# The first chunk's x copied on chip, its channels in a new order, and a new order of all tasks

## The chip, the cores and the metric

The kernel runs on one core of one Trainium2 chip. The metric is the device time of one execution in microseconds (us), taken as the median of several runs. A profile is taken of one further execution, and its time stands beside the span that the profile shows. PE is the matmul engine, PEld its loading of weights, DVE the vector engine, ACT the scalar engine, POOL the GpSimd engine, and SP the engine from whose queue the DMA transfers are issued.

## The reference

All arrays are float32. An attention with a recurrent state runs over 768 steps for 4 x 8 pairs of batch and head with 40 channels each; an MLP of 320 to 2048 to 320 follows on its 3072 tokens.

```python
for t in range(S):
    y[:, :, t] = np.einsum('bhd,bhde->bhe', rt, state)
    Sa = np.einsum('bhde,bhe->bhd', state, at)
    state_decay = state * wt[:, :, None, :] - np.einsum('bhd,bhe->bhde', Sa, bt)
    state = state_decay + np.einsum('bhd,bhe->bhde', vt, kt)
...
x = attn_out.transpose(0, 2, 1, 3).reshape(B * S, H * D)
h = x @ w_in
g = h * (1.0 / (1.0 + np.exp(-1.702 * h)))
out = g @ w_out
```

## The kernel before

**Units and chunks.** Time is cut into 12 chunks of 64 steps. One unit is one chunk of two batches with their 8 heads, so there are 24 units; units 2c and 2c+1 make chunk c. Within a chunk the recurrence is turned into matmuls of 64x64 blocks and the inverse of a triangular matrix.

**One unit.** `load_w` and `load` bring its inputs. `decay` takes logarithms and exponentials of the decays (`FT`, `GT`, `G`, `wch`). `prep` multiplies the inputs with them: `ahT` (L629), `bhT` (L631), `khT` (L634), `kh` and `bh` (L637, from the tile `time`), and makes the masked score blocks A (L648) and RV (L660). `inverse` makes the score N (L697) and inverts by five levels, each a group of matmuls `ps_level` whose result PE needs again after copies and transposes. For units 0 to 3 (`plain_level`) that is one copy of 128x768 (L794) and one transpose of 128x512 (L733) per level. For later units (`level`) it is a copy W (L761), a subtraction E (L763), a transpose ES (L712) and a spread EX (L717 on ACT, L719 on DVE or POOL). Then come the copies Tc (L807), a last transpose and spread into T, the small products `ps_Q` and `ps_T21`, and T (L840). `solve` forms `ps_B0` and `ps_B1`, the product `ps_X`, M (L917), and `ps_y` with the unit's output and its new state. From unit 2 on the state of the unit two before enters through `zr` (L855), `ps_zT` and `ps_rz`.

**From the attention to the MLP.** `decayed` (L956 to L966) multiplies the unit's output with `FT` into the tile `x`, with 40 channels in partitions 0 to 39 and 40 in 64 to 103. The MLP needs x with channels over the partitions in five blocks of 64 for both of its halves of PE. `part_with` (L971) writes `x` to a tensor in HBM with two transfers, and `get_back` (L977) reads it into both halves of `xT` with two more. `mlp` multiplies: one group `ps_up` is the product of one of five blocks k, for one of two halves m of one of four strips q of w_in. A product of either kind waits for the x of both units of its chunk. After a gelu on ACT (L1000), `ps_down` multiplies with w_out.

**Weights.** Both weight matrices arrive as float64 bits in eight pieces (`weight`, L441), four transfers each. A piece is converted by one step on ACT (L457), three on DVE (L461, L465, L469) and one on POOL (L473). Pieces 0 to 3 are w_in, and piece q serves strip q; 4 to 7 are w_out.

**What sets the order.** Nothing is scheduled at run time. Every task has a number, and the text `ORDER` (L109 to L246) lists all of them: number, engine (p PE, a ACT, d DVE, g POOL, s SP), and the PSUM bank, or for SP a window. Each engine runs its own tasks strictly in that order, so a task that waits holds up all that stand behind it on its engine. A window such as `1s4` makes a transfer wait until all but the last four transfers issued before it have landed (`transfer`, L329); 46 of 269 SP tasks carry one. Where a task may run on several engines, the letter in `ORDER` picks one. All inputs, weights and x go through SP's one queue.

**Numbers of tasks.** 413 transfers are issued on SP. On POOL run 161 products and sums, on DVE 428.

Of the kernel before, what the change touches and what calls it, by code (L numbers as in the profile page):

```python
# [109 lines left out]
0s 8s 1s4 5s 102a 7s 6s 3a 9s 157a 87p0 88p1 10s 89a1 100p2 90a0 95d 13s4 4a 11s 93d 12s 101d2 98p3 2s 94d 97d 17s 103p1 16s 96d  # L110
142p0 15s 104a1 105d1 141p2 143a0 106d 99d3 107p1 144a2 18s4 148g 132p3 108a1 109d1 155p0 45s4 149d 27s 150g 156d0 158p2 14s4
110p1 159a2 160d2 91s4 130p0 161d 19a 24s4 112d1 162p2 111a1 22d 26s4 25s 163a2 113p1 20d 131a0 152g 164d2 34s4 92a 272s 21d
165p0 114a1 151g 271s 147a 153p2 115d1 273s 166a0 167d0 116p1 23g 28a 154d2 262p0 343s 117d1 263p2 133a3 342s 264a2 118d1 168p3
36s 31d 33s 119p1 276g 169a3 170d3 35s 120d1 42s 122a1 171p2 277d 278g 121a 43s 124d1 123a1 126p3 173d2 125a1 127d3 285a 29d
128p1 172a2 44s4 286p3 30d 54s4 37a 174p2 129d1 32g 51s4 288d3 134p1 178a2 146s4 175d2 145s 265a0 135d1 176a 187p0 289d 136p1
275s4 179a2 266g 61s 38d 138d1 188a0 341s 139s 287a3 181p0 39d 185p3 40d 137a1 177a2 290p1 313d 180a2 182a0 53s4 280g 279g 274s
186a3 183p2 292d1 281p0 291a1 333p3 41g 184d2 332p1 282d0 189p2 334a3 60s4 345s 314p0 190d2 316a0 346d 355a 191p3 347d 315d0
193d3 356p2 344s2 62s 140s 194s 195s4 192d3 293p0 335a1 358d2 46a 283p3 359d 317p1 294a0 295d0 349g 318a1 284d3 360p0 269a 348d
350g 296p1 336d 361a0 362d0 319p3 383d 357a2 297a1 298d1 384p0 321p2 49d 320a3 299p1 385a0 47d 322a2 63s4 363p3 300a1 301d1
323d2 386a0 302p1 364a3 365d3 353p0 351p2 306a1 48d 267s3 207p3 52s3 307a1 305d1 208p3 50g 268s3 64a 303d1 209p3 352d2 210p3  # L120
211p3 354d0 308a1 196p2 304a 212p3 65d 197p2 213p3 72s3 214p3 70s3 270d 55a 309p1 337s3 198p2 69s4 366p0 310a1 66d 199p2 367a0
200p2 58d 468p1 201p2 368d0 469a 473s 202p2 476s 203p2 67d 387p0 477s 470a1 490d 204p2 68g 480s 339a 205p2 369p1 388d0 206a2
215p3 371d1 218p0 219p0 56d 472s4 216p3 483g 71s4 220p0 217a3 471d 81s4 221p0 482d 79s 311p2 222p0 370a1 223p0 224p0 312d2 225p0
340d 372p3 229p1 478s4 376a3 230p1 57d 378a3 324p2 560s4 377a3 59g 226p0 78s4 375a3 325d2 231p1 73a 232p1 227p0 373d3 326p2 374d
228a0 389p3 484g 479s3 327d2 338s4 240p0 529d 390a3 481g 328d2 379p3 233p1 380a3 329d 234p1 391p2 485g 241p0 556s4 392d2 80s4
242p0 393d2 74d 486p3 235p1 487d3 530p2 236p1 75d 531a2 381p3 237p1 532a2 330s4 382d3 238p1 76d 491p2 394p3 494a2 493d2 77g
239a1 243p0 395d3 82a 488p1 557s3 396p3 489d1 474a 558s4 83d 331s 251p1 492d2 495d 252p1 84d 85d 253p1 398d3 86g 559s4 548p2
244p0 703s 397d3 549a 570d 553s 245p0 496d 550a2 552s 399d 497a 254p1 551g 554a 498p3 564d 400s 568p2 565g 499a3 246p0 569d2
500d3 563g 247p0 562d 694p2 561g 255p1 248a0 401s2 249d0 475d 256p1 250s 533p3 257p1 534a3 555d 695a 571p0 535p3 573d0 258p1
574a0 698s4 501d 696a2 609d 502g 536a3 537p2 572d0 259a1 576d 566p3 538a2 702s 402p0 575g 567d3 577a 403p0 404p0 539d2 785s3  # L130
700a 405p0 706s 708d 406p0 578p3 407p0 580d3 408p0 260d1 610p2 409p0 581d 709g 410p0 611d2 411p0 612d2 503p1 707d 582g 412a0
424p2 425p2 504d1 704s2 426p2 505d1 427p2 697d 428p2 579d3 613p1 701d 429p2 614a1 583p0 430p2 584a0 506d 431p2 585d0 432p2 507a
782s2 586d 433p2 587d 446p3 434a2 508p1 588p0 509a1 447p3 590d0 589a0 510d1 261s2 413p2 511d 699s 414p2 591d 512a 783s 415p2
592g 416p2 513p0 417p2 514a0 515d0 593p1 516d 418p2 594a1 595d1 419p2 596d 420p2 517a 597d 421p2 422p2 518p0 423a2 435p1 519d0
436p1 521d0 520g 437p1 522d0 438p1 523d0 439p1 440p1 524d0 525p2 716p0 526a2 441p1 717d0 927s 442p1 718d0 527p2 443p1 719d0
444p1 528d2 598p0 721d 445a1 540p2 720d 722g 601d0 603a0 617p1 602d0 541d2 448p3 618a1 604d0 542p2 619d1 599d0 600d 615p1 705s
544d2 449p3 616a1 781s 710d 545g 711d 605p0 723p1 606a0 450p3 607p0 451p3 546s 608d0 930s 452p3 725d1 724d1 620p0 726d 543d2
727a 773p1 453p3 621d0 778s 774a 547s 754d 728p2 622p0 454d3 455d3 729d2 456s 457p3 775a1 776g 730d2 784s 786g 779a 777s 624d0
458p3 623d0 625g 731d 793p1 833d 732a 459p3 733p2 789g 460p3 626s 734a2 794d1 735d2 714p0 790g 736d 461p3 780d 737g 1009s 918p1
755p2 923s 462p3 715d0 756a2 627s 757a2 788d 463p3 738p0 787d 464p3 739a0 740d0 919a 795p2 465d3 758p0 1006s 466d3 798a2 921d  # L140
650p3 467s 759d0 920a1 651p3 924a 928s 796d2 712p1 797d2 652p3 922s 800d 799g 653p3 932d 801a 654p3 834p0 655p3 713d1 656p3
657p3 835d0 760p2 836d0 925d 658p3 761a2 659p3 762p1 660a3 741d 628p0 742d 926s 629p0 630p0 763d1 802p2 764d1 631p0 803a2 804d2
632p0 805d 633p0 806a 743p3 634p0 746d3 635p0 747d3 837p1 931g 748d3 636p0 838a1 1007s 749d3 637p0 807p2 744d3 933g 638a0 639p1
808d2 640p1 791p3 745a 809d2 672p0 810d 792d3 811a 750p2 641p1 751a2 812p3 642p1 813a3 814d3 752p2 643p1 753d2 644p1 815d 645p1
816a 765p3 839p2 766d3 646p1 840a2 647p1 817p3 648p1 818a3 819d3 767p2 820d 649a1 821d 673p0 769d2 929s 768d2 770g 822p3 934d
674p0 825a3 826a3 940p1 827a3 675p0 1151s 828a3 935d 943a1 771s 661p2 823d3 662p2 941d1 1154s 824a 663p2 942d1 997p3 945d 944g
664p2 998a 1002s 978d 938p1 946g 665p2 939d1 666p2 772s 667p2 668p2 829p1 669p2 999a3 1000d 1001s 830d1 670p2 1003a 1011d 676p0
671a2 1004d 831p3 841p1 677p0 832d3 1005s 842d1 936p3 843d1 678p0 937d3 844p2 679p0 845d2 947p1 1010g 680d0 846p3 948a1 681d0
1012d 682s 683p2 847d3 1013g 1008s 848d3 1019p0 1014g 949d1 684p2 1022a0 1230s 849d 1233s 979p3 685p2 980a3 950d 850s 1020d0
981a3 951g 1142p1 1021d0 686p2 1024d 1143a 1147s 1023d 1025g 982p3 1057d 687p2 1152s 952p0 851s 983a3 1145g 688p2 1156d 1146s  # L150
953a0 954d0 984p3 1144a1 955d 1148a 689p2 956d 985a3 1149d 986p0 690p2 987a0 1150s 988d0 957p1 691a2 863p3 958a1 692d2 864p3
959d1 865p3 693s 960d 866p3 961d 1026p0 867p3 1027a0 1028d0 868p3 1029d 1155g 869p3 1157d 1030a 1058p2 870p3 871p3 1059a2 872p3
# [97 lines left out]
def rwkv7_gelu_quick(ctx: ExitStack, tc: tile.TileContext, time_d, v_d, w_d, wc_d, ak_d, b_d, rv_d, w_in, w_out, out):  # L250
# [85 lines left out]
    def of(e):  # L336
        return nc.gpsimd if e == "POOL" else nc.vector
# [812 lines left out]
```

## Time and profile before

| | |
|---|---|
| median of 3 runs | 682.22 us (680.29 to 682.74) |
| the profiled execution | 679.49 us |
| its span from first to last instruction | 677.7 us |
| mean granted clock of PE | 0.994 |
| first matmul, first `ps_up`, last matmul's end | 3.80, 66.48, 673.8 us |
| `ps_y` of unit 0, of unit 1 (starts) | 42.00, 49.54 us |
| PE idle 0 to 66.4, and 66.4 to the end | 21.0, 7.4 us |
| DMA, queue of SP | 66.99 MB, 32.9% of 16 engines' span |

The span is less than the execution's time since the start and the end of the program lie around it. A span's busy shares are means over a head, in which the first two chunks' attention runs without any MLP beside it, and a long middle in which both are mixed. The chain that ended last is on PE for most of the span:

```profile
PE 88%; DMA 6%; DVE 2%; issue 1%; SPq 1%; ACT 1%; DVEq 0%; ACTq 0%
```

### The profile page before, as it was taken

The page shows a single profiled execution, that of the slowest core. Times are in us where ns is not written, and L with a number is a line of the kernel's source. Part 1 is how long each engine was busy: PE and PEld are TensorE (multiplying, and loading weights), DVE is VectorE, ACT ScalarE, POOL GpSimd, SP SyncE. Part 2 cuts the span into 40 slices and gives each one's busy share as a digit, 9 for nine tenths or more (in the row PEclk, how much of TensorE's full clock was granted, in tenths as well). Part 3 has the DMA queues.
Part 4 walks back from the last instruction along what each step waited for, and adds up shares of the span by engine and source line. Part 5 has one row for each costly group of instructions (what it writes and reads, how often), then busy time and mean ns, then how long its engine had stood idle before and what let it go on. Part 6 is the DMA issues. An engine that isn't in the chain of part 4 may idle for free.

```text
span 677.7 us, 42447 instructions
## 1 busy us (share of the span) xinstructions
PE 649.6 (96%) x19616; PEld 568.7 (84%) x19616; DVE 449.7 (66%) x916; ACT 329.1 (49%) x681; POOL 175.7 (26%) x201
## 2 busy tenths in 40 slices
PE   5777999999999999999999999999999999999997
PEld 4667787787999997888888899999889798799896
DVE  5777779777867668757776687868656766675001
ACT  3676745634564655654545445455344454263010
POOL 6541443324123123123113211322411421300000
PEclk9979999999999999999999999999999999999999
DMA  6875753415324314432404513513412411200200
GB/s 208 295 255 160 226 172 97 129 42 152 107 64 131 94 58 124 114 107 65 124 14 131 149 35 108 155 33 107 140 38 62 130 53 45 69 15 14 60 13 21
DMA packets 35473, 69.74 MB, mean 103 GB/s; under 512 B 5472, under 2 KB 14816, under 8 KB 35296
## 3 DMA queue, kind: packets, MB, share of 16 engines
q1 hardware_dynamic: 35216, 66.99, 32.9%
q8 instruction: 154, 2.52, 1.6%
q14 instruction: 23, 0.19, 0.1%
q10 hardware_dynamic: 80, 0.04, 0.0%
HBM read 59.15 MB, written 7.86 MB: 99 GB/s over the span
## 4 chain that ended last, share of the span: by engine, by line
PE 88%; DMA 6%; DVE 2%; issue 1%; SPq 1%; ACT 1%; DVEq 0%; ACTq 0%
PE ps_up L301 31%; PE ps_down L301 29%; PE ps_level L301 8%; PE ps_y L301 5%; PE ps_B L301 4%; PE ps_X L301 2%; PE ps_N L301 2%; PE ps_rz L301 1%; PE ps_RV L301 1%; PE ps_A L301 1%; PE ps_zT L301 1%; SPq L331 1%; DMA w_sb<-in_w_in 1%; PE ps_cum L301 1%; PE ps_T L301 1%
## 5 line engine op out<-in xcount | busy, mean ns | idle before, releaser
L301 PE MATMUL ps_up<-xT_all,w_sb 64*64 64x256 f32 x3840 | 253.3, 377 | 2.1 <-issue 1.3
L301 PE MATMUL ps_down<-w_sb,g 64*64 64x320 f32 (+1 forms) x3200 | 241.5, 419 | 0.2 <-ACT zr L879 0.2
L301 PEld LDWEIGHTS ps_up<-xT_all,w_sb 64*64 64x64 f32 x3840 | 170.8, 133 | 18.8 <-issue 2.1
L301 PEld LDWEIGHTS ps_down<-w_sb,g 64*64 64x64 f32 x3200 | 142.5, 133 | 31.6 <-issue 0.4
L1000 ACT ACTIVATE g<-ps_up 128x1024 f32<-128x1024 f32 x48 | 49.2, 1025 | 46.3 <-PE ps_up L301 45.8
L719 POOL TENSOR_TENSOR EX<-ES,quads 128x512 f32<-128x512 f32 x30 | 39.7, 1324 | 116.4 <-DVE ES L712 77.7
L761 ACT COPY W<-ps_level 128x512 f32<-128x512 f32 x56 | 32.8, 585 | 67.7 <-PE ps_level L301 66.0
L301 PEld LDWEIGHTS ps_level<-W,EX 64*64 64x64 f32 x2560 | 60.0, 134 | 5.4 <-DVE T L840 0.2
L763 DVE TENSOR_TENSOR E<-two,ps_level 128x256 f32<-128x256 f32 x80 | 33.1, 415 | 36.5 <-ACT W L761 32.3
L301 PE MATMUL ps_level<-W,EX 64*64 64x64 f32 (+1 forms) x2560 | 56.8, 217 | 0.0
L717 ACT ACTIVATE EX<-ES,quads 128x256 f32<-128x256 f32 x82 | 37.2, 501 | 31.9 <-DVE ES L712 31.3
L629 POOL TENSOR_TENSOR ak<-ak,FT 128x512 f32<-128x512 f32 x17 | 23.0, 1353 | 77.2 <-DMA ak<-in_ak 54.4
L301 PEld LDWEIGHTS ps_level<-PT,EX 64*64 64x64 f32 x1280 | 30.7, 138 | 11.5 <-DVE EX L733 3.3
L301 PE MATMUL ps_level<-PT,EX 64*64 64x64 f32 (+2 forms) x1280 | 32.5, 234 | 6.9 <-DVE EX L733 5.0
L712 DVE STREAM_TRANSPOSE ES<-E 128x256 f32<-128x256 f32 x80 | 35.3, 443 | 4.4
L301 PE MATMUL ps_y<-RV,kh 64*64 64x104 f32 (+1 forms) x768 | 35.4, 247 | 0.9 <-DVE M L917 0.9
L301 PE MATMUL ps_y<-M,bh 64*64 64x104 f32 (+1 forms) x768 | 35.5, 247 | 0.7 <-DVE M L917 0.5
L901 ACT COPY B<-ps_B 128x416 f32<-128x416 f32 (+1 forms) x35 | 17.2, 493 | 34.4 <-PE ps_B L301 34.2
L301 PEld LDWEIGHTS ps_y<-RV,kh 64*64 64x64 f32 x768 | 29.6, 133 | 3.2 <-DVE M L917 1.5
L917 DVE TENSOR_TENSOR M<-ps_X,later 128x832 f32<-128x832 f32 (+1 forms) x24 | 23.9, 995 | 10.2 <-PE ps_X L301 10.0
L301 PE MATMUL ps_B<-RV,A 64*64 64x104 f32 (+1 forms) x768 | 29.2, 252 | 0.8 <-issue 0.8
L637 POOL TENSOR_TENSOR kh<-time,G 128x320 f32<-128x320 f32 x18 | 16.2, 901 | 51.2 <-PE ps_y L301 34.6
(133 smaller groups left out, 1099.0 us busy)
## 6 DMA issues: line engine op xcount, KB each, us to landing
ak<-in_ak SPq DMA_DIRECT2D x48, 160.0 KB
rv<-in_rv SPq DMA_DIRECT2D x48, 160.0 KB
time<-in_time SPq DMA_DIRECT2D x24, 320.0 KB
xT_all<-x_dram SPq DMA_DIRECT2D x48, 160.0 KB
wc<-in_wc SPq DMA_DIRECT2D x20, 264.0 KB
logw<-in_w SPq DMA_DIRECT2D x24, 160.0 KB
RV<-in_v SPq DMA_DIRECT2D x24, 160.0 KB
b<-in_b SPq DMA_DIRECT2D x48, 80.0 KB
```

Of the source, the lines that this page charges most:

```text
L301: nc.tensor.matmul(o, lhsT, rhs, start=start, stop=True, skip_group_check=True)
L331: begun.append(queue.dma_start(dst, src).ins)
L629: plan.add(R, {"DVE": 690.0, "POOL": 1270.0, "sbuf": True}, lambda t: of(t.engine).tensor_mul(ahT(), ahT(), FT_of(i)), reads=T("ak", "FT") ...
L637: plan.add(R + 4, {"POOL": 870.0, "DVE": 490.0, "sbuf": True}, lambda t, n=n, dst=dst: of(t.engine).tensor_mul(dst(i)[:, :, :D], by_head(t ...
L712: plan.add(rank, dve(256), lambda t: nc.vector.transpose(ES(n), source(t)), writes=[key("ES", n, 6)], **reads)
L717: nc.scalar.activation(dst[:, :, h], ES(n), ACT.Copy, scale=quads[:, h, :1])
L719: of(t.engine).tensor_mul(dst, ES(n).unsqueeze(2).to_broadcast([128, 8, 2, 32]), quads.unsqueeze(1).to_broadcast([128, 8, 2, 32]))
L761: plan.add(rank, any2(512), lambda t: copy(t.engine)(tiles_of(W(n + 1)), blocks(psum(t, ""), 64)), writes=[key("W", n + 1, 5)], pair=pair)
L763: plan.add(rank, dve(256), lambda t: nc.vector.tensor_sub(tiles_of(E(n + 1)), every(two32, [128, 2, 4, 32]), blocks(psum(t, ""), 64)[:, :, ...
L901: plan.add(R, any2(4 * wide), lambda t: copy(t.engine)(dst(), some(psum(t, "")[:, :, :208])), writes=[("Bv", i)] if x and c > 0 else T("B" ...
L917: plan.add(R + 1, dve(8 * wide), lambda t: nc.vector.tensor_tensor(M_of(i)[:, :, :wide].rearrange("p (j b) n -> p b j n", b=2), some(psum( ...
L1000: plan.add(-45, {"ACT": 1030.0, "table": "gelu"}, lambda t: nc.scalar.activation(g_of(c * NQ + q).rearrange("p m r n -> p r m n"), psum(t, ...
```

## The change

Three things change together.

**Channels.** w_in's rows stand in a new order (`order`, L1120): in a block k of 0 to 3, 32 partitions hold channels 0 to 31 of head 2k and 32 those of head 2k+1, and block 4 holds what is left, channels 32 to 39 of all eight heads. So 32 of the 40 channels of `x` go to `xT` without changing their place among 32 partitions.

**x of chunk 0.** `first_x` replaces `decayed` there: two products of 128x256 in place of four of 128x128. Four tasks per unit, on DVE or ACT, copy 32 partitions x 512 numbers each from `x` to `xT` (key `xm`); only block 4, a fifth of the bytes, goes through HBM. Products with k < 4 wait for `xm`, those with k = 4 for `xs`. In the new order the copies of unit 0 run on ACT, those of unit 1 two on DVE and two on ACT. For the other chunks all of x still goes through HBM, but its write takes four transfers instead of two, since block 4 is laid out in pieces of 512 bytes.

**The order of all tasks.** `ORDER` is new from start to end. Unit 0's attention is finished first, then unit 1's; w_in's piece 1 is loaded after the others (0, 2, 3). No SP task carries a window any more. SP issues 457 transfers. Some tasks that may run on several engines move: of 161 products and sums on POOL 80 are left, of DVE's 428 there are now 533 (spreads EX and T on POOL 36 before and 3 after, on DVE 35 and 85; `ahT` on POOL 17 and 3; x of later units on POOL 9 and 0). ACT loads its tables 36 times instead of 30.

```diff
             x = x_of().rearrange("p (n f) b t -> p n b f t", f=2)
             for u, b in product(BITS, BITS):
                 at = slice(4 * u + 2 * b, 4 * u + 2 * b + 2)
-                y = both(i)[:, at, :64] if c > 0 else part(t)[:, u, 2 * b:2 * b + 2, :64]
-                of(t.engine).tensor_mul(x[:, b ^ u, b], y, FT_of(i)[:, at])
+                of(t.engine).tensor_mul(x[:, b ^ u, b], both(i)[:, at, :64], FT_of(i)[:, at])
+
+        def first_x(t):
+
+            x = x_of().rearrange("p (u f) b t -> p b u f t", f=2)
+            y, FT = (v.rearrange("p u (b f) t -> p b u f t", f=2) for v in (part(t)[:, :, :, :64], FT_of(i).rearrange("p (u j) t -> p u j t", u=2)))
+            for b in BITS:
+                nc.vector.tensor_mul(x[:, b, ::1 - 2 * b], y[:, b], FT[:, b])
...
-            plan.add(R + 6, {"DVE": 1000.0}, decayed, reads=T("FT"), writes=T("x"), pair=("y", i))
+            plan.add(R + 6, {"DVE": 800.0}, first_x, reads=T("FT"), writes=T("x"), pair=("y", i))
-        rows = lambda: drams[i].rearrange("(e d j) n -> e d (j n)", e=2, d=D)
+        rows = lambda e, k: drams[i].rearrange("(e q) (k n) -> e q k n", e=2, k=NK)[e, :, k]
+        whole, rest = (lambda e: x_of()[64 * e:64 * e + 32]), (lambda e: x_of()[64 * e + 32:64 * e + D])
...
             for e in BITS:
-                transfer(t, rows()[e], x_of()[64 * e:64 * e + D].rearrange("p j b t -> p (j b t)"))
+                if c > 0:
+                    transfer(t, rows(e, slice(0, 4)).rearrange("q k n -> q (k n)"), whole(e).rearrange("p j b t -> p (j b t)"))
+                transfer(t, rows(e, 4).rearrange("(d j) n -> d j n", j=4), rest(e).rearrange("p j b t -> p j (b t)"))
 
         def get_back(t):
             for h in HALF:
-                transfer(t, xT_of(c)[h, p].rearrange("q k n -> q (k n)"), drams[i].rearrange("(q k) n -> q (k n)", q=64))
...
+                to = xT_of(c)[h, p].rearrange("q k n -> q (k n)")
+                transfer(t, to if c > 0 else to[:, 4 * 128:], drams[i] if c > 0 else drams[i][:, 4 * 128:])
+
+        if c == 0:
+            for h, e in product(BITS, BITS):
+                plan.add(R + 6, {"DVE": 400.0, "ACT": 590.0, "sbuf": True}, lambda t, o=64 * h + 32 * e, e=e: copy(t.engine)(
+                    xT_of(c)[o:o + 32, p, :4].rearrange("q k n -> q (k n)"), whole(e).rearrange("p j b t -> p (j b t)")),
+                         reads=T("x"), writes=[("xT", c), ("xm", (c, p))])
...
-            plan.add(R + q, pe((1, 256)), go, reads=[("xs", (c, p)) for p in BITS] + [("weight", q)],
+            plan.add(R + q, pe((1, 256)), go, reads=[("xs" if c > 0 or k == NK - 1 else "xm", (c, p)) for p in BITS] + [("weight", q)],
...
-    order = [d + D * (e + 2 * j) for e in range(2) for d in range(D) for j in range(H // 2)]
+    order = [(q % 32 if k < 4 else 32 + q % 32 // 4) + D * (q // 32 + 2 * (k if k < 4 else q % 4)) for q in range(64) for k in range(5)]
```

The two orders begin so (the first lines of `ORDER`; the numbers of tasks differ from 102 on, as tasks were added):

```diff
-0s 8s 1s4 5s 102a 7s 6s 3a 9s 157a 87p0 88p1 10s 89a1 100p2 90a0 95d 13s4 4a 11s 93d 12s 101d2 98p3 2s 94d 97d 17s 103p1 16s 96d
...
+0s 5s 6s 7s 102a 8s 161a 9s 3a 1s 10s 87p0 88p1 11s 14s 12s 89a1 13s 345s 90a0 93d 94d 100p2 95d 103p3 97d 4a 96d 98p1 101d2
...
```

More of the change, by code (lines that the diff above doesn't have):

```diff
@@ L114 @@
[L114 to L121, printed above, removed]
@@ L977, in get_back @@
         def get_back(t):
             for h in HALF:
-                transfer(t, xT_of(c)[h, p].rearrange("q k n -> q (k n)"), drams[i].rearrange("(q k) n -> q (k n)", q=64))
-        plan.add(-50, {"SP": 700.0}, part_with, reads=T("x"), writes=T("xd"), size=DM * 512)
-        plan.add(-50, {"SP": 700.0}, get_back, reads=T("xd") + ([("weight", raws.index("x"))] if c in (1, 2) else []), writes=[("xT", c), ("xs", (c, p))], size=2 * DM * 512)
+                to = xT_of(c)[h, p].rearrange("q k n -> q (k n)")
@@ L984, in rwkv7_gelu_quick @@
+        plan.add(-50, {"SP": 1400.0 if c > 0 else 700.0}, part_with, reads=T("x"), writes=T("xd"), size=DM * 512 * (5 if c > 0 else 1) // 5)
+        plan.add(-50, {"SP": 700.0}, get_back, reads=T("xd") + ([("weight", raws.index("x"))] if c in (1, 2) else []),
+                 writes=[("xT", c), ("xs", (c, p))], size=2 * DM * 512 * (5 if c > 0 else 1) // 5)
     g_of = lambda n: buf("g", n, [128, 2, 2, 256])
```

264 lines of the change are left out of this document (136 added, 128 removed).

## The prediction, made before the result

> **What bounds the kernel now.** I read the page's first two parts, then the table of stretches, the waits, the groups and the timeline around the first product of the MLP.
>
> ```profile
> PE 649.6 (96%) x19616; PEld 568.7 (84%) x19616; DVE 449.7 (66%) x916; ACT 329.1 (49%) x681; POOL 175.7 (26%) x201
> PE   5777999999999999999999999999999999999997
> PEclk9979999999999999999999999999999999999999
> DMA  6875753415324314432404513513412411200200
> ```
>
> PE is the bound, except in the first four slices. The table of stretches (length, then busy us of PE, PEld, DVE, ACT, POOL, then clock, DMA share and GB/s) puts a border on it:
>
> ```profile
> 20.00:30.00 10.00, 7.60 (x310) 6.25 (x302) 8.59 (x12) 7.85 (x13) 5.52 (x3) 1.00 0.87 291
> 30.00:40.00 10.00, 7.31 (x237) 6.53 (x239) 7.50 (x14) 7.52 (x23) 5.85 (x3) 0.75 0.93 311
> 40.00:50.00 10.00, 7.75 (x323) 6.57 (x315) 7.54 (x15) 6.88 (x24) 4.16 (x5) 0.91 0.68 217
> 50.00:60.00 10.00, 7.23 (x309) 6.61 (x312) 8.35 (x18) 6.72 (x12) 2.64 (x3) 1.00 0.62 177
> 60.00:66.40 6.40, 4.81 (x244) 4.45 (x248) 4.15 (x7) 3.59 (x9) 0.00 (x0) 1.00 0.44 115
> 66.40:678.00 611.60, 604.18 (x17932) 528.70 (x17922) 403.01 (x836) 289.01 (x580) 147.23 (x147) 1.00 0.31 89
> ```
>
> After 66.4 PE lacks 7.4 us in 611.6, about 4 of them after the last matmul. So a new order can win next to nothing there and can only lose. Before 66.4 PE is busy 45.4 us of 66.4, and even that flatters it. At the rates of the dense stretches its groups there are worth 32: 17 `ps_level` at 0.85, twelve of A, N and RV at 0.47, `ps_cumc` 4 at 0.52, `ps_cum` 4 at 0.27, B 4 halves and one pair at 0.36 and 0.72 each, X 2 at 0.71, y 2 at 1.43, the rest 2. From PE's start at 3.8, some 30 us of the head are waiting. What ends the head is the first `ps_up`, and the timeline (start, us, engine) tells what it waited for:
>
> ```profile
> 52.43 0.86 DVE L962 TENSOR_TENSOR x<-ps_y,FT 128x128 f32<-128x128 f32 x4
> 56.67 0.46 SPq L331 DMA_DIRECT2D x_dram<-x  x1
> 61.39 1.09 SPq L331 DMA_DIRECT2D xT_all<-x_dram  x2
> 66.48 2.48 PE L301 MATMUL ps_up<-xT_all,w_sb 64*64 64x256 f32 x40
> ```
>
> x of unit 1 is ready at 53.3; it lies behind other transfers on SP until 56.7, is written to HBM until about 61.3, read back until about 66.4. That is 13.2 us, in which PE did only what the attention of units 2 and 3 gave it.
>
> **The change, part by part.** Whatever is moved, PE does the same groups of matmuls. So I compare the time of the first `ps_up`, and how much PE work stands ahead of it. By the new order six groups `ps_level` (0.85 each in dense stretches) and one each of A, N, B1, zT (0.47, 0.47, 0.72, 0.32) that stood ahead of it come after it: 7.1, say 7.0 us. New span = new first `ps_up` + 611.2 (677.7 - 66.48) + 7.0 + stalls that are new behind it. The change wins only if `ps_up` comes more than 7 us earlier.
>
> *To unit 0's first level.* b is issued ahead of rv and logw of unit 1 behind time, so N, which began at 11.71 after a wait for b, can start near 9. But on DVE both products with time (L637) now stand ahead of RV, PV and EX. Before they ran at 11.37, just after b; I take time's landing at 10.0 (bounds: 9, with one transfer less ahead of it, and 11.3). Then 0.48 + 0.48 + 0.68 + 0.69 + 0.65 + 0.71 = 3.7 us: the first `ps_level` at 13.8 instead of 14.91.
>
> *Unit 0's levels* no longer alternate with unit 1's. One costs PE 1.1, the ACT copy L794 0.80, the DVE transpose L733 0.71, which the trace runs one after another, with hops 2.75:
>
> ```profile
> L794 ACT COPY PT<-ps_level 128x768 f32<-128x768 f32 x15 | 11.9, 802 | 7.7 <-PE ps_level L301 5.8 <-DVE EX L733 1.2 <-ACT logw L536 0.6
> L733 DVE STREAM_TRANSPOSE EX<-ps_level 128x512 f32<-128x512 f32 x16 | 11.4, 710 | 9.9 <-ACT PT L794 8.8 <-PE ps_level L301 1.1
> ```
>
> The second level starts at 17.5 (rv of unit 1 must land for a matmul in between), the fifth at 25.6 (before: 30.83). Tc and ES in turn (5 x 0.45), the ACT spread (0.9), Q, T21 and T between weight steps of 0.8 bring X to 32.8 (before 38.63), M (1.0, behind one more weight step) to 35.7, y of unit 0 to 35.7-37.1 (before 42.0). Six us won.
>
> *Unit 1* loses them again. Its last level stands behind y of unit 0: 37.2, as before (37.42). On DVE three weight steps and x of unit 0 (39.8) stand ahead of its Tc and ES (41.2); spread to 42.1; Q, QT, T21, T to 44.1; X at 44.2-44.9 (before 48.36). Now M of unit 1 stands on DVE behind wz, bhT, zr, khT and RV of unit 2, whose exponentials ACT ends at 44.8 since it made four copies of x of unit 0 first (4 x 0.59). 0.15 + 0.75 + 0.48 + 0.80 + 0.68 = 2.9: 47.7; M to 48.7; y to 50.2. Ahead of x on DVE stand kh, P21, PV, EX, a weight step and A (0.48 + 0.41 + 0.69 + 0.71 + 0.80 + 0.68 = 3.8): 52.5.
>
> *x.* Four products of 128x128 (276 ns each) become two of 128x256. No row has that from PSUM with FT; nearest is L763, 415 ns. 0.83, no change (bounds 0.55 and 1.1). x of unit 1 is ready at 53.3, as before.
>
> *The copies.* No row copies 32x512. Bounds: 0.20 (L807, 32x64) and 0.585 (L761, 128x512 on ACT); width sets it, so 0.59. Two on DVE, two on ACT behind exponentials and logarithms that end at 53.5: 54.7. What PE still has ahead of it, B0 of unit 2 and RV of unit 3, waits for A (52.5) and is done by 53.9. First `ps_up` at 54.7, with 2 us either way for the eight waits summed.
>
> *Stalls behind it.* zT of unit 3 follows seven products (3.0 us) and needs DVE's zr, which stands behind the copies, two scans (1.4 to 1.5), B, RV, EX: 58.0 against 57.7, 0.4. The block that still goes through HBM (k = 4) is wanted after about 5.3 us, 60.0. Its write is issued at 53.3; ahead of it SP issues loads that can't go before `ps_cum` of unit 3 (48.8). By the rows, the full trip took 4.7 + 5.0 in the head and, later, 4.06 and 3.94 in the chain; a first load of 160 KB landed 2.3 after its issue. So a fifth of the bytes comes between 58.6 (issue 0.7, two trips of 2.3) and 63.0: a stall of 0 to 3. I take 0.6, nearer the small one, as these are small. Together 1.0. The Trainium skill ("DMA: Bandwidth & Descriptors", "Anatomy of one DMA — SWDGE (gpsimd) path") speaks against a large gain here: a transfer costs about 2.0 us whatever its size, so a fifth of the bytes does not take a fifth of the time. By that figure the block would land near 58.4 and the stall be nothing, 0.6 less in the sum; by the head's rows it would be 3. The first load's 2.3 agrees with it, the head's 5.0 doesn't.
>
> *Priced at nothing:* all windows on SP (46 waits for earlier transfers) go, which PE feels only through late loads (a rival below). From chunk 1 on, the write of x takes four issues for two (0.32 each, 0.7 us later); PE hides it by products of the chunk before, as only one wait of 0.6 for x stands in the trace. Spreads, `ahT` and x move from POOL to DVE: 41 + 9 spreads at 0.7, 14 ahT at 0.88, 9 x at 1.1 to 1.45, 11 QT at 0.41 come to 67, less copies W, Tc, zT and others that go to ACT or POOL, about 20; +46 us: DVE goes from 66% to 73%, POOL loses half. PE's matmuls hide it; uncovered, see C. Six more ACT table loads of 1.28 lie on an engine at 49%.
>
> Sum: 54.7 + 611.2 + 7.0 + 1.0 = 673.9 for the span, 3.8 less than 677.7. The profiled execution took 679.49, 1.8 more than its span, and the median of the runs is 682.22: 678.4.
>
> **The rivals.** *A, more is won.* The head waits for loads in the first 17 us, and POOL hardly runs beside DVE any more, which brings DVE products with two SBUF operands from 0.80 (L634) to 0.68. If time and logw land 2 us sooner and this adds 1 to 2, `ps_up` comes at 51 and the time is 674.5. Against it: 311 GB/s at 30-40 leaves little room.
>
> *B, loads too late.* Without windows everything issued lies in one queue. Weight 1's four loads and RV of unit 3 can't be issued before 48.9 and need, at 300 GB/s, till 56; ACT's L457 for weight 1 stands ahead of the zT copies, RV's product on DVE ahead of zr. At the 217 GB/s of 40-50 they land 3 us later, and the k = 4 block with them: 3 to 4 us of PE, all that was won. 682.
>
> *C, slower: DVE decides.* For units 4 to 23, E, ES, spread and ahT now queue on DVE with the rest. Each unit's five levels are a chain between DVE and PE; where it gives the next matmul late, PE stands. It decides from 0.19 us per unit (3.8 / 20); at 0.5 per unit it costs 10: 688. For it: from 100 to 120 DVE is busy 18.0 of 20 already. Against: a spread of 0.70 on DVE is shorter than 1.32 on POOL or 1.0 on ACT, and all of PE's gaps behind 66.4 but the tail sum to 3.5 us at today's 66%.
>
> **How the numbers follow.** Forecast 0.48 (own range 675 to 681.5, from 2 us either way at `ps_up` and 0 to 3 at k = 4), A 0.12, B 0.13, C 0.27. A measurement tells 0.5%, 3.4 us, from no change. Faster by that: A and 0.34 of the forecast, 0.46; within: 0.14 and B, 0.27; slower: 0.27. The range takes in A and most of C: 671 to 688.
>
> **What would show it.** First `ps_up` between 53 and 57; `ps_y` of unit 0 near 36 and of unit 1 near 49; x at 53 with DVE, not PE, in front of it; a wait of `ps_up` for xT_all under 1.5 us; after that PE short of no more than 9 us to the end. I am wrong if x of unit 1 comes before 50 or after 56, if PE's gaps behind 100 us sum to over 8, or if SP's loads end the waits at 55-62.

## The result, and the profile after

The changed kernel takes 725.86 us (median of 6 runs, 722.47 to 727.27) where the kernel before takes 681.63 beside it (680.29 to 684.85): 1.0637 times as long, with a 95% interval of 1.0603 to 1.0670. Forecast were 678.4 and a range of 671 to 688. The profiled execution has a span of 723.7 us, 46 more than before. Two kernels below each had one execution over 1.5% above their fastest (702.23 and 720.3 us), which their ratios leave out and their medians keep.

The page's first two parts, for the kernel after (busy time, share and number of instructions of each engine; then the span in 40 slices):

```profile
PE 675.0 (93%) x19616; PEld 534.9 (74%) x19616; DVE 478.8 (66%) x982; ACT 331.9 (46%) x678; POOL 96.9 (13%) x120
...
PE   6677998999999999999999999999999999999997
...
PEclk9668999999999999999999999999999999999999
DMA  7944533523312431333233322423241322201100
```

PE is still the busiest, but it is no longer the chain that ended last: that is on PE for 72% of the span, where it was 88%, and DVE has 12% of it where it had 2%:

```profile
PE 72%; DVE 12%; ACT 6%; issue 5%; DMA 4%; SPq 1%; ACTq 0%; DVEq 0%
```

The table of stretches (length, busy us of PE, PEld, DVE, ACT, POOL, granted clock, DMA share, GB/s), cut at the first product of the MLP:

```profile
20.00:30.00 10.00, 6.41 (x210) 5.58 (x213) 4.81 (x9) 2.40 (x3) 0.00 (x0) 0.76 0.92 336
30.00:40.00 10.00, 7.99 (x212) 7.24 (x211) 7.09 (x12) 5.76 (x11) 0.00 (x0) 0.56 0.59 201
40.00:50.00 10.00, 6.90 (x244) 5.67 (x240) 7.80 (x19) 8.13 (x23) 7.27 (x3) 0.78 0.47 129
50.00:60.00 10.00, 7.37 (x225) 6.73 (x221) 6.87 (x9) 4.04 (x12) 3.39 (x4) 0.53 0.45 162
63.50:723.70 660.20, 632.07 (x18280) 496.55 (x18280) 435.83 (x906) 299.60 (x597) 74.56 (x70) 1.00 0.29 83
```

Behind the first product PE now lacks 28 us in 660, where it lacked 7.4 in 611.6. That is still too kind, since a matmul that waits inside a group counts as busy. In what follows I use the **excess** of a group of matmuls: the time from its start to that of the next group, less what such a group takes in dense stretches (0.43 for a product `ps_up`, 1.08 for `ps_down`, 0.47 for a level, and so on; all groups together 641.2 us). From 100 to 650 us the excess sums to 44.1 us after the change and to 4.0 before it.

Around the first product, the timeline (start, us, engine):

```profile
61.22 0.74 DVE L968 TENSOR_TENSOR x<-ps_y,FT 128x256 f32<-128x256 f32 x2
...
61.99 1.46 SPq L331 DMA_DIRECT2D x_dram<-x  x2
62.00 1.26 ACT L993 COPY xT_all<-x 32x512 f32<-32x512 f32 x2 [0.20 <-DVE x L968]
62.00 1.40 DVE L993 COPY xT_all<-x 32x512 f32<-32x512 f32 x2
...
63.55 2.70 PE L301 MATMUL ps_up<-xT_all,w_sb 64*64 64x256 f32 x40 [0.78 <-DVE xT_all L993]
```

The copies do what they are for: 1.6 us from x to the first product instead of 13.2. But x of unit 1 is ready only at 62.0, 8.7 later than before, and the first product starts 2.9 us earlier with 7.0 us less work ahead of it. So in these two profiles the head has lost 4, and some 40 are lost behind it. (Three kernels below run the same tasks up to the first product; there it starts at 60.5, 60.9 and 63.2, so some 3 of the 4 may be chance.) The waits of PE behind 66 us show no single culprit:

```profile
PE ps_N L301 <- issue: 2.3, 2, 2.1
PE ps_level L301 <- issue: 1.9, 3, 1.1
PE ps_up L301 <- DMA xT_all<-x_dram: 1.7, 3, 0.7
PE ps_level L301 <- DVE EX L719: 1.7, 6, 0.4
PE ps_B L301 <- issue: 1.4, 2, 0.7
PE ps_up L301 <- DVE E L763: 1.2, 1, 1.2
PE ps_Q L301 <- DVE T L719: 1.0, 2, 0.6
```

These are many short waits, at levels, at Q, at products that stand behind such a step or wait for DVE's E, from which they need only its bank of PSUM. Three causes offered themselves: the places in the new order (O), the engines (C, on record as a rival), and the head's delay (H).

### The profile page after: what moved, and what is told of

Same layout as the page of the kernel before. It is cut to its first block, busy times and chain, and to the rows that moved or that the text cites. A ratio compares the mean times of both kernels' runs of the same rounds, so it can differ in the third digit from the quotient of the medians.

```text
span 723.7 us, 42428 instructions
## 1 busy us (share of the span) xinstructions
PE 675.0 (93%) x19616; PEld 534.9 (74%) x19616; DVE 478.8 (66%) x982; ACT 331.9 (46%) x678; POOL 96.9 (13%) x120
## 4 chain that ended last, share of the span: by engine, by line
PE 72%; DVE 12%; ACT 6%; issue 5%; DMA 4%; SPq 1%; ACTq 0%; DVEq 0%
PE ps_up L301 23%; PE ps_down L301 22%; PE ps_level L301 9%; PE ps_y L301 4%; PE ps_B L301 4%; PE ps_X L301 2%; DVE ES L712 2%; PE ps_rz L301 2%; ACT W L761 2%; PE ps_A L301 2%; PE ps_N L301 1%; ACT Tc L807 1%; DVE E L763 1%; DMA xT_all<-x_dram 1%; DVE Tc L807 1%
## 5 line engine op out<-in xcount | busy, mean ns | idle before, releaser
L301 PEld LDWEIGHTS ps_up<-xT_all,w_sb 64*64 64x64 f32 x3840 | 152.3, 133 | 36.1 <-issue 3.3
L301 PEld LDWEIGHTS ps_down<-w_sb,g 64*64 64x64 f32 x3200 | 129.8, 134 | 48.0 <-issue 2.8
L301 PEld LDWEIGHTS ps_level<-W,EX 64*64 64x64 f32 x2560 | 53.4, 134 | 17.2 <-issue 6.1
L301 PE MATMUL ps_level<-W,EX 64*64 64x64 f32 (+1 forms) x2560 | 55.7, 219 | 3.2 <-DVE EX L719 1.7
L719 DVE TENSOR_TENSOR EX<-ES,quads 128x512 f32<-128x512 f32 x70 | 50.7, 724 | 2.2
L1046 DVE TENSOR_TENSOR ob<-ob,ps_down 128x320 f32<-128x320 f32 (+1 forms) x25 | 11.7, 469 | 49.1 <-ACT ob L1044 49.0
L807 ACT COPY Tc<-ps_level 32x64 f32<-32x64 f32 x110 | 22.4, 203 | 44.9 <-PE ps_level L301 23.5
L717 ACT ACTIVATE EX<-ES,quads 128x256 f32<-128x256 f32 x56 | 25.5, 502 | 36.9 <-DVE ES L712 35.8
L301 PEld LDWEIGHTS ps_level<-PT,EX 64*64 64x64 f32 x1280 | 32.7, 146 | 10.7 <-DVE EX L733 4.5
L301 PE MATMUL ps_y<-RV,kh 64*64 64x104 f32 (+1 forms) x768 | 35.7, 251 | 2.0 <-DVE M L917 0.7
L1044 ACT COPY ob<-ps_down 128x320 f32<-128x320 f32 (+1 forms) x20 | 8.3, 413 | 56.6 <-PE ps_down L301 49.5
L637 POOL TENSOR_TENSOR bh<-time,G 128x320 f32<-128x320 f32 x19 | 18.6, 977 | 94.0 <-issue 58.9
L301 PEld LDWEIGHTS ps_B<-RV,A 64*64 64x64 f32 x768 | 25.3, 135 | 7.3 <-ACT Tc L807 1.4
```

The source lines that it names most:

```text
L301: nc.tensor.matmul(o, lhsT, rhs, start=start, stop=True, skip_group_check=True)
L637: plan.add(R + 4, {"POOL": 870.0, "DVE": 490.0, "sbuf": True}, lambda t, n=n, dst=dst: of(t.engine).tensor_mul(dst(i)[:, :, :D], by_head(t ...
L717: nc.scalar.activation(dst[:, :, h], ES(n), ACT.Copy, scale=quads[:, h, :1])
L719: of(t.engine).tensor_mul(dst, ES(n).unsqueeze(2).to_broadcast([128, 8, 2, 32]), quads.unsqueeze(1).to_broadcast([128, 8, 2, 32]))
L807: copy(t.engine)(dst, src[:, u, :, f])
L1044: plan.add(-45, any2(wide), lambda t: copy(t.engine)(ob(), psum(t, "")[:, 0, :wide]), writes=[("ob", serial + n)], pair=("down", serial + n))
```

## The experiments

Orders are put together from the two lists: a task of one list is found in the other by what it computes, banks of PSUM are given anew where a seam needs it. Some of these kernels have their lines shifted by 4 or 5.

**One part alone.** The new channels, the four writes and the copies in the old order:

```diff
-138d1 192a0
+138d1 139a 140a 141a 142a 192a0
...
-197d3 364p2
+197d3 198d 199a 200a 201d 364p2
```

> The order, the engines and the windows of the kernel before, with the other two parts of the change alone: channels in their new order, four writes of x from chunk 1 on, and chunk 0's x copied on chip (the four copies of a unit right behind its x). If the loss of 44 us lies in the new order of the tasks (theory O), these parts are harmless: x of unit 1 is ready at 53.3 as before, its copies end near 55, the first ps_up comes at 55 to 58, the products with k = 4 wait till about 62, and some 3 to 5 us of the 11 between 55 and 66 are won: 676 to 681. If the copies or the four writes cost what is lost (theory X, later transfers of x for every chunk), it takes over 695 and many waits of ps_up for xT_all stand in the trace. 682 within 2 would mean that the copies change nothing, as the block that goes through HBM sets the pace.

689.65 us against 681.18: 1.0134 (1.0089 to 1.0179). Neither the gain nor a stalled middle: the excess from 100 to 650 is 7.6, that ahead of the first product 37.1 instead of 30.6.

**The two orders cut at a seam and put together crosswise**, each part with its own engines and windows.

```diff
-ORDER = new
+ORDER = new[:410] + [t for t in old if t not in new[:410]]
```

> The changed kernel up to the point that its profile reaches at 113 us (410 tasks), and from there on what is left in the order of the kernel before, with that one's engines and windows. By the excess of PE's tasks over steady work, the changed kernel is some 9 us behind the old order at the seam and loses 35 more behind it. Theory O (the new order starts matmuls too soon behind the work they need, all along) and theory C (DVE has too much to do, as the engines moved) both expect 688 to 694: the early loss stays and the later one is gone. Theory H (the head comes out of step, and all that follows stalls because units 2 and 3 start late) expects 715 to 726.

697.21: 1.0213 (1.0152 to 1.0274), from executions of 691 to 702 us.

```diff
-ORDER = new
+ORDER = old[:430] + [t for t in new if t not in old[:430]]
```

> The other way round: the order of the kernel before with the copies of chunk 0 up to the point that its profile reaches at 106 us (430 tasks), then what is left in the new order with the new engines and no windows. Theories O and C: the loss of the middle is there without the new head: 682, less the 0 to 5 that the copies win, plus 35: 710 to 718. Theory H: 677 to 688.

718.63: 1.0551 (1.0503 to 1.0599). With the first experiment the four corners are there, and they add up:

| | old rest | new rest |
|---|---|---|
| old start, with the copies | 689.65 | 718.63 |
| new start | 697.21 | 725.86 |

The new rest costs 29.0 behind the old start and 28.7 behind the new one; the new start costs 7.6 and 7.2, within some 5 either way by the intervals. So H falls: the middle stalls whichever head it follows. From 681.2 on: 8.5 for channels, writes and copies, 7.6 for the new start, 28.7 for the new rest; 44.8, with 44.2 measured.

**The engines put back.** 325 tasks run on another engine than before; each goes back, here five spreads:

```diff
-382a 510a 515d 525d 528d
+382d 510g 515a 525a 528g
```

> The changed kernel's order, task by task, but every task runs on the engine that it had in the kernel before (spreads, ahT, x and W0 back to POOL and ACT, as there; 96.9 us of POOL become some 175 again). Theory C (the spreads and products moved to DVE make it late) expects most of the 35 us behind 100 back: 685 to 695. Theory O (the place in the order, not the engine, is what is too early) expects 715 to 735, since spreads on POOL take 1.32 where DVE takes 0.70 and the order leaves them no more time.

742.48: 1.0909 (1.0864 to 1.0954), 17 us slower still. The waits of PE behind 66 us in that kernel:

```profile
PE ps_level L305 <- POOL EX L723: 4.3, 5, 1.2
PE ps_level L305 <- DVE EX L723: 2.8, 5, 0.8
PE ps_T L305 <- ACT QT L830: 2.0, 1, 2.0
```

Behind 66 us the spreads on POOL are now what is waited for most. The reverse, new engines in the old order:

```diff
-382d 510g 515a 525a 528g
+382a 510a 515d 525d 528d
```

> The old order with the copies (689.65 in the first set), but with the engines that the changed kernel uses for every task: 46 us more on DVE, POOL at half. Theory C in its pure form (DVE has too much to do): 705 or more, with most of the stalls at E, ES and EX on DVE. Theory O (it is the places in the order): 684 to 697, since spreads on DVE are shorter than on POOL and the old order leaves DVE's results a median of 1.0 us before PE wants them at a level, where the new order leaves 0.56.

705.10: 1.0369 (1.0302 to 1.0437), 15.5 us slower than the same order with its own engines, at the edge of what C had asked for, and its longest waits behind 75 us are levels for a spread on DVE (4.7 us). Each order goes with its own engines, and changing them costs 15 to 17 us either way. So more work on DVE does harm where the order wasn't made for it, but it isn't what loses the 29 us of the new order, where the moves help.

**Channels and writes alone in the old order, and the copies elsewhere** (with a second buffer for x).

```diff
-                if c > 0:
+                if True:
                     transfer(t, rows(e, slice(0, 4))...
-            reads=[("xs" if c > 0 or k == NK - 1 else "xm", (c, p)) ...
+            reads=[("xs", (c, p)) ...
```

> The order, engines and windows of the kernel before; of the change only the channels in their new order, x of unit 0 and 1 made in two products instead of four, and the write of x in four transfers (for all chunks, also the first); no copies on chip. If the 8.5 us that the old order with the copies lost are due to where the copies stand on ACT (theory P), this is the time of before within 2: 679 to 684. If four writes, or the new layout in HBM, delay x everywhere (theory X), 685 to 690, with waits of ppm for x in the middle.

688.25: 1.0121 (1.0059 to 1.0184). Nearly all of the 8.5 is there without any copy ("ppm" in the text stands for `ps_up`).

```diff
-46a 291p3
+46a 139a 140a 141a 142a 291p3
...
-393a0 47d 330a2
+393a0 199a 200a 47d 198d 201d 330a2
```

> The old order with the copies of chunk 0 again, but at places where ACT and DVE stood idle in the profile of before (unit 0's four behind the weight step that ends at 52.4, unit 1's two on ACT at 61 and two on DVE at 62), and with a second buffer for x, so that x of unit 1 need not wait for them. Theory P (the copies right behind x held up ACT, which had the copies B and the spread of unit 1 behind them: one wait of 3.9 and another of 1.5 in the head): first ps_up at 65 to 67 and 679 to 684 in all, since the matmuls ahead of the first product are set by the chains of units 2 and 3 and not by x. Theory X (copies or writes cost it wherever they stand): 687 to 692.

685.43: 1.0080 (1.0046 to 1.0114). At these places the copies cost nothing that can be told from the channels alone, but they win nothing either: the first product starts at 70.3, behind the matmuls that the old order puts ahead of it.

**The windows** (eight of the 46).

```diff
-1s 13s 14s 345s 275s 18s 34s 44s
+1s4 13s4 14s4 345s3 275s3 18s4 34s4 44s4
```

> The changed kernel, with the windows of the kernel before put back on the same 46 transfers. In the changed kernel PE stood at 19.9, 26.2 and 56.5 us for 1.8, 1.7 and 2.1 us at a place 256 instructions apart each (the 193rd of 256), while the DMA engines were busy all the time; the kernel before has six such gaps of over 0.5 us in all, the changed one fourteen (16 us against 6, counting all that these places take). Theory W (loads without windows fill the DMA engines, and PE's own program arrives late): the gaps in the head shrink below 1 us, and 3 to 8 us are won: 717 to 723. Theory B as it was on record (loads land too late without windows) would also win some, but at waits for rv, logw or weights. Theory O: the stalls in the middle stay, 25 to 30 us. 724 to 728 or more would say that the windows play no part, or that holding loads back costs what it wins.

724.27: 1.0661 (1.0582 to 1.0740), not to be told from the changed kernel. In the head two gaps on PE go, though. PE's timeline of the changed kernel:

```profile
17.70 0.63 PE L301 MATMUL ps_N<-b,ak 40*64 40x64 f32 x26
19.92 0.28 PE L301 MATMUL ps_N<-b,ak 40*64 40x64 f32 x3 [1.59 <-issue]
...
24.24 0.49 PE L301 MATMUL ps_level<-PT,EX 64*64 64x96 f32 x10
26.23 1.07 PE L301 MATMUL ps_level<-PT,EX 64*64 64x96 f32 x19 [1.50 <-issue]
```

and the same two groups with windows:

```profile
17.32 0.65 PE L306 MATMUL ps_N<-b,ak 40*64 40x64 f32 x32
...
23.82 1.50 PE L306 MATMUL ps_level<-PT,EX 64*64 64x96 f32 x32
```

A group of matmuls that has all its data stops in its middle, "issue", for 1.5 us, and with windows it doesn't. Both gaps stand at the 193rd of a block of 256 instructions of PE. Five more profiles of kernels whose start has no windows have both too, each 1.1 to 1.7 us, so the windows, and not chance, take them away. First `ps_up` comes at 62.0, which is within the 60.5 to 63.6 of the profiles with the same tasks there and no windows; later gaps, up to 1.5 us, remain.

**PE given something to do in its waits.** 63 products move ahead; for one, product 218 ahead of level 374:

```diff
-314a1 311d1 374p3 315d1
+314a1 311d1 218p2 374p3 315d1
```

> The changed kernel with 63 products of the MLP moved ahead in the order, each to stand in front of a matmul of the attention (or of another product) that waited 0.2 us or more in the profile of the changed kernel behind 62 us; a product was taken only if what it reads was there before that wait began, from the next 13 tasks of PE. The waits sum to 44.4 us, and those products are worth 28.1 of them. Theory O (a matter of places on PE alone: DVE and ACT could keep up if PE only had something to do meanwhile): most of it is kept, 698 to 710. Theory D (the chain of a unit through DVE and ACT itself is the bound, so a product put in front of one wait is missing in front of the next): 716 to 728, with about as many waits as before, at other places.

721.77: 1.0581 (1.0510 to 1.0652). Of 28 us filled 4 at most were kept (the interval takes in the changed kernel's 1.0637), and the excess from 100 to 650 is 44.2, as it was. O in its simple form falls: filling PE's waits does not help. What a product fills in front of one matmul is missing in front of the next, as D said.

**What bounds the new order: the chain or the amount of work on DVE.** Counting from the starts of `ps_N` and `ps_Q`, the inverse of units 4 to 21 takes 34.4 us on the mean in the new order and 42.7 in the old, and fewer of them run side by side: two at a time for 157 of the 495 us from 105 to 600, where it was 316; one or none for 338, where it was 179. Three kernels test it:

```diff
-  tiles_of(E(n + 1)), every(two32, [128, 2, 4, 32]), blocks(psum(t, ""), 64)[:, :, :, :32]
+  tiles_of(E(n + 1))[:, :, :, :4], every(two32, [128, 2, 4, 32])[:, :, :, :4], blocks(psum(t, ""), 64)[:, :, :, :4]
```

> The changed kernel with the subtraction E cut to an eighth: of each block of 32 columns it writes the first 4 (the rest of the tile stays zero), so the inverse is left incomplete. 80 such steps of 0.42 us fall to some 0.15: 20 us less, each on the chain level, E, ES, EX, level of one unit. In the changed kernel only 1.25 units on the mean stand between N and Q from 105 to 600 us (1.64 before), and none or one alone in 338 of 495 us (179 before). Theory K (that chain is the bound wherever PE waits, since too few units overlap): 10 to 18 won, 708 to 716. Theory M (the amount of work on DVE, in whatever place): some 10 to 20 won as well, so this run alone does not tell them apart.

```diff
-            for u, b in product(BITS, BITS):
+            for u, b in [(0, 0)]:
                 at = slice(4 * u + 2 * b, 4 * u + 2 * b + 2)
```

> The changed kernel with a quarter of the product that makes x of units 2 to 23 (one of four parts; the rest of x stays what it was), which no chain of an inverse waits for: 66 steps of 0.29 us, 19 us of DVE left out, about as much as E in the run beside it. Theory M (DVE has too much work): as much won as there, 706 to 716. Theory K (the chain of the inverse, not DVE's amount of work): 0 to 6 won, 720 to 727.

> The kernel before with the same cut of E, as a control: 20 us less on DVE and in the chains. There PE is the bound behind the head and its waits after 100 us sum to some 6: 0 to 3 won, 678 to 682, whatever holds for the new order. If it won 10 or more, the old order would be bound by its chains too, and the reading of the profile of before (PE is the bound) would be wrong.

E cut in the new order: 715.78, 1.0440 (1.0362 to 1.0518), some 13 us better than the changed kernel's 1.0637. x cut: 722.40, 1.0565 (1.0496 to 1.0634), 5 better, not clear of noise. The executions that count lie at 709 to 717 and at 718 to 725 us. E cut in the old order: 681.83, 0.9985 (0.9955 to 1.0015), nothing. The stretch from 105 to 600 us, where the number of matmuls (the x of PE) tells how far the work got in 495 us; first the kernel before:

```profile
105.00:600.00 495.00, 492.82 (x15142) 430.95 (x15137) 351.36 (x731) 247.36 (x506) 130.59 (x139) 1.00 0.31 91
```

the changed kernel:

```profile
105.00:600.00 495.00, 475.31 (x14117) 378.95 (x14113) 356.97 (x751) 242.88 (x498) 55.33 (x61) 1.00 0.32 90
```

the changed kernel with E cut:

```profile
105.00:600.00 495.00, 479.66 (x14508) 387.87 (x14503) 350.58 (x770) 246.72 (x504) 56.80 (x63) 1.00 0.32 90
```

and with x cut:

```profile
105.00:600.00 495.00, 476.34 (x14220) 381.22 (x14216) 347.56 (x699) 242.24 (x495) 55.32 (x61) 1.00 0.32 89
```

The changed kernel does 1025 matmuls less in this time than the kernel before; at 32.7 ns each (641.2 us over 19616) that is 33.5 us. DVE is no busier in it, 357 against 351 us of 495, though for 7% less of the program, so its total is not what PE runs into. Over the whole run the cut of E takes 17 us off DVE's busy time (478.8 to 461.6), all in the chain, and brings 391 matmuls back; the cut of x takes 13 off (to 465.7), beside the chain, and brings 103. By the excess from 100 to 650 it is 33.7 us with E cut, 43.7 with x cut and 44.1 without. (The profile with E cut is its kernel's fastest execution, 709.18, which flatters its figures.) What x won, and some 3 us of what E won, came from the head, where these kernels still run the tasks of the changed one, so by chance. K is shown for some 10 us, which this cut brings: there the chain holds PE. How much more of the 40 hangs on it these runs do not tell.

That it does so because fewer inverses overlap was my reading of the two counts, and the same traces speak against it. With the excess of this stretch sorted by how many are under way, the changed kernel loses 15 of the 157 us with two (9%) and 28 of the 338 with one or none (8%); the kernel before loses 3 of its 179 with one alone (2%). What differs is how close the order puts two successive levels of one unit. In units 4 to 23 the work that PE has from the start of one level to the next is worth 4.0 us on the median in the new order, 4.7 in the old, and under 3.5 us in 27 of 80 pairs against 5. Those 27 have 3.0 us of work on the mean and took 3.4; together they came 10 us late, with E cut 5, with x cut 9. The kernel with the 63 products moved has 28 such pairs, so it did not test this. No kernel changed this distance alone. Nor are the levels all of it: of some 43 us of excess in the stretch, 8 stand in front of a level and 17 in front of products of the MLP.

**What the 8 us of the channels are.** Up to 44 us the kernel with the channels alone has the instructions of the kernel before, and still its unit 0's y was 1.4 late, behind a gap on PE. Chance, or the channels?

```diff
     for t in tasks:
         t.fn(t)
+    for _ in range(64):
+        nc.gpsimd.memset(starts[:, :, 0], 0.0)
```

> The kernel before with 64 small memsets added on POOL behind all its tasks, where POOL has nothing to do; nothing else differs. It asks where the 8 us of the run with the channels alone come from: that kernel's instructions up to 44 us are those of the kernel before, yet unit 0's y came 1.4 later, behind a gap of 2.1 us on PE at 31.7 us, at the first instruction of a block of 256 of PE's program (0.56 at the same instruction before). Theory L (which of PE's blocks arrive late hangs on how the program lies in memory or on chance, not on the channels): a head unlike the one before, 683 to 690, or a gap of over 1.5 us near 31. Theory X (the channels and four writes do it): 681 within 2, and the gap at 31 under 0.8.

> The kernel before itself, for a second profile of its head. Theory L in the form of chance: the gap at 31 us differs from the 0.56 of the first profile by more than 0.8, and unit 0's y from 42.0 by more than 1. If the program's place decides, or the channels do: both within 0.3.

The padded kernel takes 683.11, 1.0012 (0.9978 to 1.0046): no change; one further execution of the kernel before took 686.07, where 13 runs beside it went from 677.98 to 687.78. In the two heads the gap at 31 us is 1.6 and 1.3 us (0.56 in the first profile), unit 0's y is at 43.6 and 43.8 (42.0), x of unit 1 at 55.7 and 55.4 (53.3). The first product starts at 69.2 and 69.9 (66.5). So chance moves the head by 2 to 3 us, and I had read one of the luckier profiles. That explains the gap at 31, but not a median 7 to 8 higher.

```diff
-                transfer(t, rows()[e], x_of()[64 * e:64 * e + D]...)
+                for q in (slice(0, 32), slice(32, D)):
+                    transfer(t, rows()[e][q], x_of()[64 * e + q.start:64 * e + q.stop]...)
```

> The kernel before, old channels and all, but its write of x to HBM takes four transfers instead of two (each half split into its first 32 partitions and its last 8); nothing else. The channels with four writes cost 7 to 8 us in the old order (688.25), of which the profile shows some 4 in the head and a gap of 1.9 us on PE at 132 us. Theory S (the two further issues on SP's one queue, 24 times 0.7 us, and what they push back, cost it): 685 to 690. Theory Y (the new layout in HBM with its pieces of 512 bytes, or the products of 128x256 for the first x): 681 within 2.

684.37: 1.0036 (1.0002 to 1.0070). Between the two theories: four issues for two cost some 2.4 us, with an interval of 0 to 5. What is left, some 3 to 7 by the kernels with the new channels, belongs to the layout in HBM with its small pieces, or to x of chunk 0; which of them was not tried. In three of the four kernels with the new channels in the old order a gap of 1.9 us on PE near 132 us comes back; neither profile of the kernel before has it, nor the padded one, and the one with four writes has 1.1 at 128.

## Why the prediction was wrong, by its steps

- **PE bounds the kernel before, and a new order can only lose behind 66 us**: right. Cutting E there changed nothing.
- **"Stalls that are new behind it", 1.0 us**: the step that failed most. In the sum's own form, 723.7 = 63.55 + 611.2 + 7.0 + 42.0. I looked at two stalls near the first product and took it that the rest of the new order would keep PE fed as the old one does, though the list of its tasks was there to be read. 29 us of it are the new rest, by the crosswise orders. There the chain level, E, ES, EX, level sets the pace for a part, 10 us by the cut of E; by the traces the new order leaves too little of PE's other work between two levels. What makes the remainder is open.
- **Rival C** (0.27, 688) had the mechanism, a chain between DVE and PE that gives the next matmul late, and even named the price from which it decides. Its cause was wrong: not the spreads moved to DVE, which help the new order by some 17 us, but, as far as the traces tell, the places in the order. It was also priced too low: 0.5 us per unit against 28.7 / 20, 1.4. And the range's upper end, 688, took in no more than C's 10 us.
- **The head**: the first level at 13.0 (forecast 13.8), then 39.7 for y of unit 0 (35.7), 57.6 for y of unit 1 (48.7), 62.0 for x (53.3), 63.55 for the first product (54.7). Some 3 us of these 9 may be chance: with the same tasks, two other profiles have y of unit 1 at 54.0 and 54.4 and the first product at 60.5 and 60.9. Three things were left out. PE stood for its own program at 19.9, 26.2 and 56.5 us, 5.6 us in gaps; the third is missing in two of the three other profiles with these tasks. PE's granted clock fell, which the last section takes up. And ahead of M of unit 1, zr and khT were put at 0.75 and 0.80; they took 1.56 and 1.35 while POOL ran L629 and L637. That repeats in four more profiles of this order, and where POOL is idle the same two lines take 0.44 to 0.49 and 0.66 to 0.69 in the changed kernel. DVE's and then POOL's timeline:

```profile
49.63 1.56 DVE L855 TENSOR_TENSOR zr<-zraw,wz 128x320 f32<-128x320 f32 x1
51.11 1.35 DVE L634 TENSOR_TENSOR ak<-ak,GT 128x512 f32<-128x512 f32 x1
...
52.98 1.01 DVE L917 TENSOR_TENSOR M<-ps_X,later 128x832 f32<-128x832 f32 x1
```

```profile
49.04 1.79 POOL L629 TENSOR_TENSOR ak<-ak,FT 128x512 f32<-128x512 f32 x1
50.80 1.11 POOL L637 TENSOR_TENSOR bh<-time,G 128x320 f32<-128x320 f32 x1
```

- **The copies and the new product**: right in size. On ACT a copy took 0.62 (forecast 0.59), on DVE 0.41 and 0.98; the two products for x 0.74 together (0.83).
- **k = 4**: a stall of 0.6 was forecast, and none came. PE paused for 1.2 us shortly ahead of the first such product, which starts at 70.50, but in the middle of the group before it, at a block of its program:

```profile
68.80 0.62 PE L301 MATMUL ps_rz<-rv,zT 40*64 40x64 f32 x25 [0.20 <-ACT zT L868]
70.37 0.34 PE L301 MATMUL ps_rz<-rv,zT 40*64 40x64 f32 x7 [0.96 <-issue]
70.50 1.86 PE L301 MATMUL ps_up<-xT_all,w_sb 64*64 64x256 f32 x28
```

  In three profiles with the same head PE does not wait there either; only with windows does that product wait for x from HBM, 1.4 us. (By the text's own terms, two trips of 2.0 give 58.0, not 58.4.)
- **"Priced at nothing"**: the windows, right in the total (724.27), so rival B is out. The four writes, wrong: 2.4 us by themselves, 5 to 9 with the new channels in three kernels (1.0080 to 1.0134). The moves of engines, wrong where the order stays (15.5), and mis-sized: the terms given come to 65 at most, not 67, and DVE's busy time grew by 29 us (449.7 to 478.8), not 46, and stayed at 66%. The six table loads were not tried.
- **The signs named beforehand** came true: x of unit 1 after 56, and PE short of far more than 8 us behind 100 (21 us without a matmul from 100 to 700).

## What to carry to other kernels

Where nothing is scheduled at run time, a new order of all tasks is a change of its own, and here, with its engines, it was the largest, 36 of 45 us. Before it is priced at nothing, count from the two lists how much other work stands between the dependent steps of one chain, and hold that against the time that the steps take. A count that fits the loss, as that of the overlapping inverses did, is worth one more table: does the loss fall where the count says? Costs of engines and an order belonged together here, so neither could be judged by moving it alone. And a forecast in single microseconds for a head needs more than one profile of it.

## What the runs showed of the hardware

PE can stand for its own instructions. The page's third part lists the queue that brings them (packets, MB, share):

```profile
q8 instruction: 154, 2.52, 1.5%
```

That is 16,384 bytes a packet, and of the 39,513 rows of PE one packet per 256. The gaps at the 193rd place of each 256 (what lies over 0.1 us from row to row) sum to 16.4 us in the changed kernel and to 6.2 and 12.1 in the two profiles of the kernel before, 11.3 in that of its padded copy; other places have a median of 0.7 and 0.5. The times of the packets bear it out. In the changed kernel, at each of the 14 gaps of over 0.5 us, the last packet had ended 1.2 to 1.6 us before PE went on; at the other blocks the median is 2.2. What makes a packet late is not settled. The gaps at 19.9 and 26.2 stand where the DMA engines are 92 to 100% busy and go with the windows, but the longest, 2.1 us at 56.5, stands where they are 10% busy (55 to 60 us). The Trainium skill ("Runtime: NRT & Kernel Launch", section "Instruction fetch mechanics") says that instructions are refilled in blocks of 256 and that crossing into the next is mostly hidden. The trace agrees with the first, and with the second for most blocks: 14 of 154 held PE for over 0.5 us.

The granted clock in the changed kernel's head went down to 0.53 and 0.56 (50 to 60, 30 to 40 us), where the kernel before has 0.75 at the least, though PE ran fewer matmuls there (681 from 30 to 60 us, against 869). Three more profiles with the same head have 0.79 on the mean from 20 to 60 us, where this one has 0.66 and the kernel before 0.91. The matmuls show it: at a clock of 1.0 the groups of `ps_y` start 0.18 us apart, at 0.5, in y of unit 1, 0.34.

```profile
40.07 0.35 PE L301 MATMUL ps_y<-RV,kh 64*64 64x104 f32 x8
40.25 0.35 PE L301 MATMUL ps_y<-M,bh 64*64 64x104 f32 x8
...
57.59 0.70 PE L301 MATMUL ps_y<-RV,kh 64*64 64x104 f32 x8
57.93 0.70 PE L301 MATMUL ps_y<-M,bh 64*64 64x104 f32 x8
```

An estimate from such paces, over all matmuls that follow one another without a pause while the clock is down: ahead of the first product PE took 8 us longer for its work in the changed kernel, 5 in the three others with its head, 2 in the kernel before. No run changed the clock alone, and how much of it lay on the chain to the first product is open.
